# Gated attention, routed experts and a dense layer on one core: the attention's last tiles reordered, embeddings used unscaled, expert weights loaded earlier

## The chip, the cores and the metric

The kernel runs on one core of a Trainium2 chip. The metric is the device time of one execution in microseconds (us), the median of several runs.

## What is computed

The reference has three stages, each feeding the next. Inputs are float32.

```python
# 1. gated recurrent attention: 4 batches x 8 heads, 768 steps, head dim 48
for t in range(S):
    state = alpha[:, :, t, :, None] * state + einsum('bhd,bhe->bhde', k[:, :, t], v[:, :, t])
    y[:, :, t] = einsum('bhd,bhde->bhe', q[:, :, t], state)
x = y.transpose(0, 2, 1, 3).reshape(3072, 384)
# 2. one of 8 experts per token, by cosine
xn = x / (norm(x) + 1e-6); en = expert_emb / (norm(expert_emb) + 1e-6)
logits = xn @ en.T / tau
idx = argmax(logits, 1); gate = softmax(logits)[arange(N), idx]
for e in range(8):                                   # w1: 384 x 1024, w2: 1024 x 384
    m = idx == e; out[m] = gate[m, None] * (maximum(x[m] @ w1[e], 0) @ w2[e])
# 3. dense layer, 384 -> 2048 -> 384, with ELU
h = out @ w_in; g = where(h > 0, h, exp(minimum(h, 0)) - 1); y = g @ w_out
```

## The kernel before, in words

**Attention** (`attention()`, L287) works on 24 tiles: 6 chunks of 128 steps times 4 batches, all heads of a tile together. A tile goes through stages that are pipelined over the loop of `fast()` (L714 on). `stR` (L333) and `stA` (L346) are two scans of the gates on VectorE (DVE), each followed by a product on GpSimd (POOL): Kh (L344) and Qh (L353). `stS` (L372) makes scores on TensorE (PE, 16 matmuls, L381), `stP` (L383) masks them on DVE in two halves, `stT` transposes Kh, `stC_state`, `stC_carry` and `stC_values` make the product with the carried state (L408), the new state (L434) and the product with the values (L426); ScalarE (ACT) evicts. `stD` (L457) multiplies the tile's rows with a matrix rhsX that holds an identity and the expert embeddings, so that one pass gives the token rows and their logits; ACT copies the rows and sums their squares, and DVE reduces the logits (L469; the reduce is kept in a list `late`). In turn `i` of the loop stand: the loads of tile i+4 on SP's queue, the scores of i+1, the scans of i+2, the masks of i+1, pending routing steps (`step(5)`, `step(7)` take up to 12 from a list `todo`), the rows of i-1 and the state and value products of i. PE, DVE, ACT and POOL take their instructions in the order in which the program writes them.

**Start.** `fast()` loads the tiles' gates (`at`), q and k in one piece (`qk`), v, the constants (`cs`), the embeddings (`emb_t`) and the matrix `sel` from which rhsX is broadcast. The embeddings are normed by 15 small steps (`inv_norm1`, L129: two on DVE, then twelve Newton steps and an addition on ACT, L140 to L148, with reciprocals on DVE at L705 and L732), scaled on ACT (L733, L734), transposed on PE (L762) and copied into rhsX (L763), in turn 0.

**Routing.** The tiles form six groups (0 to 5, 6 to 11, 12 to 15, 16 to 19, 20 and 21, 22 and 23). For a group, `stR1` (L495) takes maximum, one-hot and counts of the logits on DVE, with the inverse norm of the rows (`inv_norm`, L106) beside it; `stR2` (L547) turns counts into row numbers by small matmuls (L553 to L557) and three DVE steps; `stX` and `gates` make the softmax weight; `put` (L578) scales a tile's rows on ACT (L574, L575) and scatters them by an indirect DMA of POOL (L584) into a buffer `xs` in DRAM, sorted by expert.

**Weights.** The expert weights come in pieces of 128 x 512. `load_w` loads one, `split_piece` (L189) splits it into a high part (ACT, L201) and a low part (DVE, L204). Twelve pieces, expert 0's whole weight, are loaded and split during attention, from tile `WAIT` on; the low parts of eight of them are put off (`spare`, run by `split_spare`). The dense layer's weights are 64-bit words, loaded by `load_d` and decoded by `decode` (L228) on DVE, ACT and POOL during the expert stage.

**Ending.** After turn 21, `ending()` (L808) writes out by hand the order of the last tiles, the last groups' routing, the packing of the counts, the test of the decays and the first expert's input: tiles 22 and 23 are put straight into its first layer by a product with one-hot columns (`first_x`, L592), the other rows are read back from `xs` on SP's queue (`load_rows`) and transposed (`turn`, L967, L982).

**Experts** (`moe1`, L955): 8 experts of 8 blocks, one first-layer product and one second-layer product per block; after the first two blocks a branch (L1058) chooses the common path by a number that all engines read. Behind it stand `load_d(0)`, `load_d(1)`, `load_x(1)`. The last block's `mm2` evicts its outputs to `x2T` (L1041, L1042, L1045) and splits the first 512 columns for the dense layer in between (`split_x`, L1103). **Dense layer** (`moe2`, L1151): 6 units of 512 tokens, 16 blocks each: h (L1187) into one of four PSUM banks, then minimum, exp, ELU and the split into gh and gl on DVE and ACT (L1189 to L1197), then the output product (L1208 to L1210), which for the last term needs gl.

Of the kernel before, what the change touches and what calls it, by code (L numbers as in the profile page):

```python
# [8 lines left out]
F32 = mybir.dt.float32  # L9
# [31 lines left out]
WAIT = 10  # L41
# [18 lines left out]
CONST = [("ident", 128), ("tri", 128), ("dec", E), ("base", E), ("tok", NT), ("key", E), ("cap", E), ("iota", E)]  # L60
# [3 lines left out]
def fused_kernel(ctx, tc, qk, a, v, emb, w12, wi, wo, cst, sel, cols, out):  # L64
# [38 lines left out]
    ss = const.tile([128, NT], F32, name="ss")  # L103
    tick = const.tile([1, 1], F32, name="tick")
# [24 lines left out]
    def inv_norm1(pool, x):  # L129

        shape = [x.shape[0], 1]
        y = pool.tile(shape, F32, name="rs_y1")
        t = pool.tile(shape, F32, name="rs_t1")
        h = pool.tile(shape, F32, name="rs_h1")
        yi, vec, act = y.bitcast(I32), nc.vector, nc.scalar
        first = [
            lambda: vec.tensor_scalar(yi, x.bitcast(I32), 1, None, op0=ALU.logical_shift_right),
            lambda: vec.tensor_scalar(yi, yi, -1.0, float(0x5F3759DF), op0=ALU.mult, op1=ALU.add),
        ]
        steps = [lambda: act.activation(out=h, in_=x, func=AF.Copy, scale=-0.5)]  # L140
        for _ in range(3):
            steps += [
                lambda: act.activation(out=t, in_=y, func=AF.Copy, scale=h),
                lambda: act.activation(out=t, in_=t, func=AF.Copy, scale=y),
                lambda: act.activation(out=t, in_=t, func=AF.Copy, bias=1.5),
                lambda: act.activation(out=y, in_=t, func=AF.Copy, scale=y),
            ]
        steps += [lambda: act.activation(out=y, in_=y, func=AF.Copy, scale=x, bias=1e-6)]  # L148
        return y, first, steps

# [23 lines left out]
    def split_spare(n):  # L174

        for _ in range(n):
            if spare:
                spare.pop(0)()
# [10 lines left out]
    def split_piece(lag=None):  # L189
# [13 lines left out]
        def low_part():  # L203
            nc.vector.tensor_tensor(l[:, sl], r, h[:, sl].bitcast(F32), op=ALU.subtract)  # L204
# [82 lines left out]
    def attention():  # L287
        with ExitStack() as st:
# [27 lines left out]
            def load(i):  # L316
# [3 lines left out]
                at[i], qkt[i] = ats[i % LB], qks[i % LB]  # L320
# [136 lines left out]
            def stD(i, keep=False):  # L457
# [23 lines left out]
                if keep:  # L481
                    late.pop()()
# [181 lines left out]
            def fast():  # L664
# [38 lines left out]
                for f in guess:  # L703
                    f()
# [632 lines left out]
```

## Time and profile before

| | |
|---|---|
| runs | 796.0, 794.42, 794.0 us; median 794.42 |
| profiled execution | 795.59 us, span 793.8 us |
| PE busy | 770.1 us, 97% of the span |
| DVE busy | 522.2 us, 66% |
| ACT busy | 362.6 us, 46% |
| POOL busy | 188.9 us, 24% |
| granted TensorE clock | 0.992 of full speed on the whole |
| DMA | 76.25 MB, 96 GB/s over the span |

The span is the time between the first and the last instruction of the profiled execution; the execution's own time is 1.79 us longer. Attention takes the first 130 us or so, its ending reaches to 160, the experts to 385, the dense layer to the end. Busy shares are means over these stages. In a timeline, the bracket behind an instruction says how long its engine stood idle before it and what the profile names as the releaser.

### The profile page before, as it was taken

What the parts mean: (1) busy time and instruction counts of PE and PEld (TensorE: products, weight loads), DVE (VectorE), ACT (ScalarE), POOL (GpSimd) and SP (SyncE); (2) the same over time, 40 slices, a digit from 0 to 9 for tenths busy, and PEclk for the clock granted to TensorE, in tenths of its full rate; (3) what the DMA queues carried; (4) which work ended last, traced back from release to release, by engine and by line L of the source; (5) the groups of instructions that cost most, each with busy time, mean ns of one, the idle gap of its engine ahead of it and who ended that gap; (6) DMA issues with size and microseconds to landing.
All of it is one profiled execution on the core that took longest, in us unless ns stands there. A gap on an engine that the chain in (4) does not pass through costs nothing.

```text
span 793.8 us, 13698 instructions
## 1 busy us (share of the span) xinstructions
PE 770.1 (97%) x5077; PEld 699.1 (88%) x5077; DVE 522.2 (66%) x1001; ACT 362.6 (46%) x802; POOL 188.9 (24%) x222
## 2 busy tenths in 40 slices
PE   7999998899999999999999999999999999999996
PEld 4888887489999999999898899999999999999996
DVE  6789999846877877896576755454555545545442
ACT  4667877435455455554545433333333323323231
POOL 5545667322333433342000020020002002002002
PEclk9899999999999999999999999999999999999999
DMA  9998773366665666661000010010001001001001
GB/s 245 245 259 205 233 202 92 109 176 201 185 198 184 204 198 204 213 200 35 1 1 1 1 40 1 0 40 1 1 1 40 1 1 40 1 0 41 1 1 40
DMA packets 44804, 76.25 MB, mean 96 GB/s; under 512 B 11958, under 2 KB 21302, under 8 KB 44734
## 3 DMA queue, kind: packets, MB, share of 16 engines
q1 hardware_dynamic: 41662, 65.89, 29.5%
q0 software_dynamic: 3072, 9.45, 3.3%
q8 instruction: 40, 0.66, 0.4%
q14 instruction: 30, 0.25, 0.1%
HBM read 63.12 MB, written 12.22 MB: 95 GB/s over the span
## 4 chain that ended last, share of the span: by engine, by line
PE 40%; issue 30%; DVE 3%; POOL 3%; ACT 2%; POOLq 0%; ACTq 0%
PE h L1187 6%; PE y L1031 5%; PE y L1033 4%; PE y L1032 4%; PE h L1000 4%; PE h L1001 4%; PE h L999 4%; POOL out_dram L1221 2%; PE o L1210 2%; PE o L1208 2%; PE o L1209 2%; PE t L980 1%; DVE dlo L260 1%; DVE g L1193 1%; DVE mn L1189 1%
## 5 line engine op out<-in xcount | busy, mean ns | idle before, releaser
L1189 DVE TENSOR_SCALAR mn<-h 128x512 f32<-128x512 f32 x96 | 66.2, 690 | 139.7 <-PE h L1187 139.7
L1190 ACT ACTIVATE mn<-mn 128x512 f32<-128x512 f32 x96 | 60.7, 632 | 171.7 <-DVE mn L1189 163.2
L1210 PE MATMUL o<-dwo,gl 128*128 128x384 f32 x384 | 129.4, 337 | 1.4 <-DVE gl L1197 1.4
L1209 PE MATMUL o<-dlo,gh 128*128 128x384 f32 x384 | 128.4, 334 | 0.0
L1208 PE MATMUL o<-dwo,gh 128*128 128x384 f32 x384 | 128.2, 334 | 0.0
L1187 PE MATMUL h<-xh,dwi 128*128 128x512 f32 x288 | 112.8, 392 | 0.6 <-ACT x2T L1045 0.6
L1187 PE MATMUL h<-xh,dlo 128*128 128x512 f32 x288 | 113.2, 393 | 0.0
L1187 PE MATMUL h<-xl,dwi 128*128 128x512 f32 x288 | 112.5, 392 | 0.0
L1221 POOL DMA_INDIRECT out_dram<-ob,ids x24 | 23.2, 965 | 340.8 <-ACT ob L1218 337.1
L1196 ACT ACTIVATE gh<-g 128x512 fp32r<-128x512 f32 x96 | 60.7, 633 | 77.9 <-DVE g L1193 77.9
L1003 ACT ACTIVATE hh<-h 128x432 fp32r<-128x432 f32 (+6 forms) x64 | 32.4, 506 | 107.1 <-PE h L1001 98.9
L204 DVE TENSOR_TENSOR wlo<-raw,whi 128x512 fp32r<-128x512 f32 x96 | 72.8, 786 | 5.6 <-ACT whi L201 5.6
L1193 DVE SCALAR_TENSOR_TENSOR g<-mn,h 128x512 f32<-128x512 f32 x96 | 66.1, 688 | 15.2 <-ACT mn L1190 14.7
L1208 PEld LDWEIGHTS o<-dwo,gh 128*128 128x128 f32 x384 | 72.0, 187 | 4.2
L1209 PEld LDWEIGHTS o<-dlo,gh 128*128 128x128 f32 x384 | 72.0, 187 | 4.0
L1210 PEld LDWEIGHTS o<-dwo,gl 128*128 128x128 f32 x384 | 72.2, 188 | 2.1 <-DVE gl L1197 1.7
L1004 DVE SCALAR_TENSOR_TENSOR hl<-h,hh 128x432 fp32r<-128x432 f32 (+6 forms) x64 | 36.7, 574 | 48.8 <-ACT hh L1003 47.4
L1031 PE MATMUL y<-hh,whi 128*128 128x432 f32 (+6 forms) x192 | 68.3, 356 | 0.0
L999 PE MATMUL h<-xh,whi 128*128 128x432 f32 (+6 forms) x192 | 66.5, 346 | 0.7 <-ACTq L1058 0.7
L244 POOL TENSOR_SCALAR dg<-dg 128x384 f32<-128x384 f32 x32 | 41.7, 1304 | 106.3 <-ACT dg L243 106.1
L1197 DVE TENSOR_TENSOR gl<-g,gh 128x512 fp32r<-128x512 f32 x96 | 65.7, 684 | 1.2 <-ACT gh L1196 1.1
L1001 PE MATMUL h<-xh,wlo 128*128 128x432 f32 (+6 forms) x192 | 66.4, 346 | 0.0
(217 smaller groups left out, 1508.9 us busy)
## 6 DMA issues: line engine op xcount, KB each, us to landing
raw<-in_w_dram SPq DMA_DIRECT2D x96, 256.0 KB
qk<-in_qk_dram SPq DMA_DIRECT2D x40, 192.0 KB
raw<-in_wi_dram SPq DMA_DIRECT2D x16, 384.0 KB
raw<-in_wo_dram SPq DMA_DIRECT2D x16, 384.0 KB
vt<-in_v_dram SPq DMA_DIRECT2D x24, 192.0 KB
xr<-xs SPq DMA_DIRECT2D x7, 576.0 KB
at<-in_alpha_dram SPq DMA_DIRECT2D x40, 99.0 KB
xs<-zero SPq DMA_DIRECT2D x7, 288.8 KB
```

The source lines that it names most:

```text
L204: nc.vector.tensor_tensor(l[:, sl], r, h[:, sl].bitcast(F32), op=ALU.subtract)
L999: nc.tensor.matmul(ps, wh, xh[:, kk], start=(kk == 0), stop=False)
L1001: nc.tensor.matmul(ps, wl, xh[:, kk], start=False, stop=(kk == KD - 1))
L1031: nc.tensor.matmul(acc[e][d], wh, hh, start=(f == 0), stop=False)
L1187: nc.tensor.matmul(ps, l, x, start=(n == 0), stop=(n == len(terms) - 1))
L1189: nc.vector.tensor_scalar(mn, ps, 0.0, None, op0=ALU.min)
L1190: nc.scalar.activation(out=mn, in_=mn, func=AF.Exp)
L1193: nc.vector.scalar_tensor_tensor(g, mn, -1.0, ps, op0=ALU.add, op1=ALU.max)
L1197: low.append(lambda: nc.vector.tensor_tensor(gl, g, gh.bitcast(F32), op=ALU.subtract))
L1208: nc.tensor.matmul(o_, gh[:, sl], wh, start=(f == 0), stop=False)
L1209: nc.tensor.matmul(o_, gh[:, sl], wl, start=False, stop=False)
L1210: nc.tensor.matmul(o_, gl[:, sl], wh, start=False, stop=(f == M - 1))
```

## The change

At the start the embeddings come unscaled as part of `sel` and go into rhsX with it; `emb`, its norm and its transposes go. The norm of the embeddings and 1/tau are made later (squares of rhsX on ACT and a sum by a matmul with ones at tile 2, one reduce and 16 more DVE steps put into `todo` at tile 5), and each group's logits are multiplied by them (`en`) in `stR1`. The loads are reordered and q and k of tile 0 split; in the first four turns the scan A stands ahead of both masks. `WAIT` goes from 10 to 9. `ending()` has a new order. Two of the last seven spare low parts stay on DVE and five go to POOL. In `moe1`, `load_x(1)` is issued ahead of the loads of the 64-bit weights, their decoding starts two blocks later, and the first dense input is split ahead of the last block's `mm2`. In `moe2`, h uses the three banks of `psG`, which stays open, in place of its own four; the first block's products are no longer reordered. The core of the diff:

```diff
-WAIT = 10
+WAIT = 9
...
-    def inv_norm1(pool, x):
...
-    def split_spare(n):
+    def split_spare(n, eng=None):
 
         for _ in range(n):
             if spare:
-                spare.pop(0)()
+                spare.pop(0)(eng)
...
-        def low_part():
-            nc.vector.tensor_tensor(l[:, sl], r, h[:, sl].bitcast(F32), op=ALU.subtract)
+        def low_part(eng=None):
+            (eng or nc.vector).tensor_tensor(l[:, sl], r, h[:, sl].bitcast(F32), op=ALU.subtract)
...
-                y = ys[i] = psG.tile([128, NP, T], F32, tag="g", name="psY") if i == NT - 1 else ps1.tile([128, NP, T], F32, name="psY")
+                y = ys[i] = psG.tile([128, NP, T], F32, tag="g", name="psY") if i == NT - 2 else ps1.tile([128, NP, T], F32, name="psY")
...
                 nc.scalar.activation(out=sq, in_=rows, func=AF.Square, accum_out=ss[:, i:i + 1])
-                if keep:
-                    late.pop()()
...
                 ops = [
+                    lambda: nc.vector.tensor_tensor(l, l, en.to_broadcast(s3), op=ALU.mult),
                     lambda: nc.vector.tensor_reduce(mx, l, axis=AX.X, op=ALU.max),
...
+                if g == NG - 3:
+                    return pz[:, 128:128 + 8 * E].rearrange("p (n e) -> p n e", e=E)
...
             def fast():
...
-                emb_t = sm.tile([E, 2 * NP * HP + 1], F32, bufs=1, name="emb_t")
-                load(0)
+                ones_f = wk.tile([128, 128], F32, bufs=1, tag="ones_f", name="ones_f")
+                esq = sm.tile([128, NP, E], F32, bufs=1, name="esq")
+                es = sm.tile([128, E], F32, bufs=1, name="es")
+                load(0, True)
+                load_a(1)
+                load_k(1)
                 nc.sync.dma_start(out=cs, in_=cst)
-                nc.sync.dma_start(out=emb_t, in_=emb)
-                load(1)
+                load_a(2)
                 load_v(0)
-                load(2)
-                nc.sync.dma_start(out=rhsX, in_=sel[:, None, :].to_broadcast([128, NP, CW + E]))
+                load_k(2)
+                nc.sync.dma_start(out=rhsX, in_=sel)
                 load_v(1)
                 load(3)
                 load_v(2)
...
-                rows, rtau = emb_t[:, :2 * NP * HP], emb_t[:, 2 * NP * HP:]
-                es = sm.tile([E, 1], F32, name="es")
-                esq = wk.tile([E, 2 * NP * HP], BF16, bufs=1, tag="junk", name="esq")
-                en, guess, newton = inv_norm1(sm, es)
+                nc.gpsimd.memset(ones_f, 1.0)
                 for j in range(2):
                     stR(j)
                     stA(j)
                     stH(j)
-                    if j == 0:
-                        stE(j)
-                        nc.scalar.activation(out=esq, in_=rows, func=AF.Square, accum_out=es)
+                    stE(j)
                 stS(0)
                 stT(0)
-                warm(ps1, "psY", 4)
-                for f in guess:
-                    f()
-                nc.vector.reciprocal(rtau, rtau)
-                stE(1)
+                warm(ps1, "psY", 6)
                 stP(0, 0)
                 stP(0, 1)
-                for f in newton:
-                    f()
+                inv, norms = inv_norm(sm, es)
+                norms += [
+                    lambda: nc.vector.reciprocal(c["tau"], c["tau"]),
+                    lambda: nc.vector.tensor_tensor(en[:, 0], inv, c["tau"].to_broadcast([128, E]), op=ALU.mult),
+                ]
...
                     stR(i + 2)
-                    stP(i + 1, 0)
-                    if i == 0:
-                        nc.vector.reciprocal(en, en)
-                        nc.scalar.activation(out=rows, in_=rows, func=AF.Copy, scale=en)
-                        nc.scalar.activation(out=rows, in_=rows, func=AF.Copy, scale=rtau)
-                    stA(i + 2)
-                    stP(i + 1, 1)
+                    if i < B:
+                        stA(i + 2)
+                        stP(i + 1, 0)
+                        stP(i + 1, 1)
+                    else:
+                        stP(i + 1, 0)
+                        stA(i + 2)
+                        stP(i + 1, 1)
+                    if i == 5:
+                        todo.append(lambda: nc.vector.tensor_reduce(es, sums, axis=AX.X, op=ALU.add))
+                        todo.extend(norms)
...
                         m, n = stR1(last[i - 2])
+                        todo.append(m.pop(0))
...
                     if i == 0:
-                        eT = psD.tile([128, NP, E], F32, tag="psX", name="eT")
-                        for p in range(NP):
-                            nc.tensor.transpose(eT[:, p], rows[:, p * 128:(p + 1) * 128], c["ident"][:E, :E])
-                        nc.scalar.activation(out=rhsX[:, :, CW:CW + E], in_=eT, func=AF.Copy)
+                        warm(psD, "psX", 3)
+                    if i == 2:
+                        nc.scalar.activation(out=esq, in_=rhsX[:, :, CW:CW + E], func=AF.Square)
+                        nc.tensor.matmul(pz[:, 64:64 + NP * E], ones_f, esq.rearrange("p n e -> p (n e)"), start=True, stop=True)
+                        sums = pz[:, 64:64 + NP * E].rearrange("p (n e) -> p e n", n=NP)
...
             def ending():
...
                     put(putq.pop(0))
+                stC_state(i)
+                stS(i + 1)
+                stC_values(i)
                 stD(i - 1)
-                stS(i + 1)
+                late.pop(0)()
+                run(todo)
+                todo.clear()
+                x3 = stX(g3)
                 stP(i + 1, 0)
                 stP(i + 1, 1)
                 late.pop(0)()
-                r = stR2(g2 - 1)
-                run(todo, r)
-                todo.clear()
-                stC(i)
-                x3 = stX(g2 - 1)
-                split_spare(2)
-                run(x3 + gates(g2 - 1), late)
-                late.clear()
-                gated.add(g2 - 1)
+                stC_state(i + 1)
+                stD(i, True)
+                r = stR2(g3)
+                stC_values(i + 1)
+                run(x3 + gates(g3), r)
+                gated.add(g3)
+                late.pop(0)()
+                for _ in range(2):
+                    put(putq.pop(0))
+                stD(i + 1, True)
                 m2, n2 = stR1(g2)
                 run(m2, n2)
-                for _ in range(2):
-                    put(putq.pop(0))
-                stC(i + 1)
-                stD(i, True)
+                late.pop(0)()
                 r = stR2(g2)
                 x2 = stX(g2)
-                run(r, x2 + gates(g2))
-                split_spare(1)
-                stD(i + 1, True)
                 while putq:
                     put(putq.pop(0))
+                run(r, x2 + gates(g2))
                 warm(ps1, "psY", 8)
                 for j in GROUPS[g2]:
                     put(j)
+                split_spare(1)
                 xr = xr_p.tile([128, 4, DM], F32, name="xr")
                 load_rows(xr, 0, [0, 128, 256, DM], puts[:-1])
...
-                split_spare(5)
+                split_spare(2)
+                split_spare(5, nc.gpsimd)
                 return xr, t0
...
                     y = acc.pop(e)
-                    if e == E - 1:
-                        for nm in ("xh2", "xl2"):
-                            first.append([stage.tile([128, U], F32R, tag="raw", name=nm) for _ in range(KD)])
                     nc.scalar.activation(out=x2T[:, 0, bass.ds(o1, n)], in_=y[0], func=AF.Copy)
                     nc.vector.tensor_copy(x2T[:, 1, bass.ds(o2, n)], y[1])
-                    if first:
-                        split_x(x2T, *first, 0, 0)
                     nc.scalar.activation(out=x2T[:, 2, bass.ds(o1, n)], in_=y[2], func=AF.Copy)
-                    if first:
-                        split_x(x2T, *first, 0, 1)
-                        split_x(x2T, *first, 0, 2)
...
+                load_x(1)
                 load_d(0, dc)
                 load_d(1, dc)
-                load_x(1)
...
+                    if n == len(blocks):
+                        for nm in ("xh2", "xl2"):
+                            first.append([stage.tile([128, U], F32R, tag="raw", name=nm) for _ in range(KD)])
+                        for kk in range(KD):
+                            split_x(x2T, *first, 0, kk)
                     if n >= LAG:
                         mm2(*blocks[n - LAG])
...
-                    j = (n - 2) * 4 // 7
-                    if j >= 0 and j != (n - 3) * 4 // 7:
+                    j = (n - 4) * 3 // 5
+                    if j >= 0 and j != (n - 5) * 3 // 5:
                         decode(j, dc, dense)
...
-            psH = st.enter_context(tc.tile_pool(name="psH2", bufs=4, space=PS))
...
-                ps = psH.tile([128, U], F32, name="h2")
+                ps = psG.tile([128, U], F32, tag="g", name="h2")
...
-                if u == f == 0:
-                    terms = [terms[n] for n in (0, 1, 3, 4, 6, 7, 2, 5, 8)]
```

## Rows read from the trace of the kernel before

**Rows 1.** Busy time by stretch; after each engine (x) instructions; then clock, DMA share, GB/s

```profile
0.00:20.00 20.00, 15.78 (x118) 9.51 (x119) 12.62 (x24) 9.25 (x28) 10.71 (x21) 0.93 0.95 244
...
120.00:165.00 45.00, 37.46 (x341) 28.29 (x339) 36.27 (x163) 24.74 (x77) 22.65 (x36) 0.96 0.41 126
165.00:384.00 219.00, 218.81 (x1203) 211.47 (x1203) 163.54 (x274) 107.84 (x217) 74.26 (x64) 1.00 0.57 173
...
390.00:450.00 60.00, 58.63 (x293) 52.15 (x292) 41.42 (x71) 29.98 (x58) 0.20 (x1) 1.00 0.05 1
```

**Rows 2.** Timeline, 7 to 24 us: start, duration, engine, line, [idle before <-releaser]

```profile
7.21 1.25 DVE L341 TENSOR_TENSOR_SCAN R<-at,pz 112x528 f32<-112x528 f32 x1 [0.89 <-DMA at<-in_alpha_dram]
...
8.45 1.16 PE L381 MATMUL psS<-Qh,Kh 48*128 48x128 f32 x16
...
11.36 1.23 DVE L341 TENSOR_TENSOR_SCAN R<-at,pz 112x528 f32<-112x528 f32 x1
...
14.90 0.15 DVE L732 RECIPROCAL rs_y<-rs_y 8x1 f32<-8x1 f32 x1 [1.42 <-ACT rs_y L148]
14.98 1.25 DVE L351 TENSOR_TENSOR_SCAN A<-at,pz 112x528 f32<-112x528 f32 x1
...
17.65 2.08 PE L381 MATMUL psS<-Qh,Kh 48*128 48x128 f32 x16 [0.53 <-POOL Qh L353]
...
22.29 1.94 PE L426 MATMUL psY<-P,vt 128*64 128x128 f32 x16
```

**Rows 3.** Waits, 38 to 54 us: total us, times, longest

```profile
DVE P L388 <- PE psS L381: 4.3, 3, 1.4
```

**Rows 4.** DVE groups by form, 55 to 130 us: busy us, mean ns

```profile
L518 DVE TENSOR_TENSOR lg<-lg,rs_y 128x48 f32<-128x48 f32 x2 | 1.2, 606 | 0.1
...
L119 DVE TENSOR_TENSOR rs_t<-rs_t,rs_y 128x6 f32<-128x6 f32 x6 | 1.0, 161 | 0.1
```

**Rows 5.** Timeline of POOL and of DVE around one tile

```profile
85.42 1.27 POOL L353 TENSOR_TENSOR Qh<-qk,A 112x512 f32<-112x512 f32 x1 [0.87 <-DVE A L351]
...
86.29 0.47 DVE L509 TENSOR_TENSOR e__1387<-lg,mx 128x48 f32<-128x48 f32 x1
```

**Rows 6.** Timeline of PE, the ending of attention and the start of the experts

```profile
135.84 0.19 PE L553 MATMUL psR<-base,ident 128*128 128x32 bf16 x1 [1.48 <-DVE lg L469]
...
136.09 1.42 PE L408 MATMUL psY<-Qh,G 48*64 48x128 f32 x16
137.44 1.98 PE L426 MATMUL psY<-P,vt 128*64 128x128 f32 x16
...
140.72 1.09 PE L426 MATMUL psY<-P,vt 128*64 128x128 f32 x16
...
150.49 3.17 PE L596 MATMUL t<-hot,xt 128*128 128x432 f32 x8 [1.40 <-ACT xt L574]
...
160.32 0.46 PE L999 MATMUL h<-xh,whi 128*128 128x432 f32 x1
...
164.78 0.47 PE L999 MATMUL h<-xh,whi 128*128 128x432 f32 x1 [0.67 <-ACTq L1058]
```

**Rows 7.** Timeline of POOL, the same stretch

```profile
141.82 0.95 POOL L584 DMA_INDIRECT xs<-xt,pos_i  x1 [4.39 <-ACT xt L575]
...
149.95 1.04 POOL L584 DMA_INDIRECT xs<-xt,pos_i  x1 [0.23 <-issue]
...
159.25 0.96 POOL L584 DMA_INDIRECT xs<-xt,pos_i  x1 [8.18 <-DVE xl L1022]
```

**Rows 8.** Timeline of DVE, the same stretch

```profile
154.07 3.08 DVE L204 TENSOR_TENSOR wlo<-raw,whi 128x512 fp32r<-128x512 f32 x5
158.02 0.61 DVE L1022 TENSOR_TENSOR xl<-t,xh 128x432 fp32r<-128x432 f32 x1 [0.88 <-ACT xh L1021]
```

**Rows 9.** Timeline, 383 to 392 us, and the page's group of L1210

```profile
386.39 0.50 PE L1187 MATMUL h<-xh,dwi 128*128 128x512 f32 x1 [0.59 <-ACT x2T L1045]
...
L1210 PE MATMUL o<-dwo,gl 128*128 128x384 f32 x384 | 129.4, 337 | 1.4 <-DVE gl L1197 1.4
```

More of the change, by code (lines that the diff above doesn't have):

```diff
@@ L103, in fused_kernel @@
     ss = const.tile([128, NT], F32, name="ss")
+    en = const.tile([128, 1, E], F32, name="en")
     tick = const.tile([1, 1], F32, name="tick")
@@ L127, in inv_norm @@
         return y, steps
-    def inv_norm1(pool, x):
[L131 to L149, printed above, removed]
     wq = [(e, s) for e in range(E) for s in range(FB * FW // SLOT)]
@@ L314, in seg, with load, load_a @@
                 return t.rearrange("c (p t) -> c p t", t=TP)
-            def load(i):
+            def load(i, apart=False):
+                load_a(i)
+                load_k(i, apart)
+            def load_a(i):
                 if i >= NT:
@@ L319, in load, with load_k @@
                 cc, b = divmod(i, B)
-                at[i], qkt[i] = ats[i % LB], qks[i % LB]
-                for t, src in ((at[i], a), (qkt[i], qk)):
-                    for r in [slice(0, C2)] if i < LB else [slice(0, D), slice(HP, C2)]:
-                        nc.sync.dma_start(out=t[r], in_=src[cc, r, b])
+                at[i] = ats[i % LB]
+                for r in [slice(0, C2)] if i < LB else [slice(0, D), slice(HP, C2)]:
+                    nc.sync.dma_start(out=at[i][r], in_=a[cc, r, b])
+            def load_k(i, apart=False):
+                if i >= NT:
+                    return
+                cc, b = divmod(i, B)
+                t = qkt[i] = qks[i % LB]
+                for r in [slice(0, C2)] if i < LB else [slice(0, D), slice(HP, C2)]:
+                    for n in [slice(1, 2), slice(0, 1)] if apart else [slice(0, 2)]:
+                        nc.sync.dma_start(out=t[r, n], in_=qk[cc, r, b, n])
             def load_v(i):
@@ L1254, in fused_kernel @@
     psG = shared.enter_context(tc.tile_pool(name="psG", bufs=3, space=PS))
-    xr_p = shared.enter_context(tc.tile_pool(name="xr", bufs=1, side="right"))
+    rest = ExitStack()
+    xr_p = rest.enter_context(tc.tile_pool(name="xr", bufs=1, side="right"))
     x0 = attention()
@@ L1259, in fused_kernel @@
         first, dense = moe1(x2T, *x0, es)
-        shared.close()
+        rest.close()
         with tc.manual_schedule():
             moe2(x2T, first, dense)
+        shared.close()
 _OUTS = [((N, DM), "float32")]
@@ L1307, in _layout @@
         "cap": np.broadcast_to(np.array(CAPS)[None, :], (128, E)),
+        "tau": np.broadcast_to(np.asarray(inputs["moe_tau"], np.float32).reshape(1, 1), (128, 1)),
         "iota": np.broadcast_to(np.arange(E)[None, :], (128, E)),
```

18 lines of the change are left out of this document (8 added, 10 removed).

## The prediction

> **What bounds the kernel now.** I read the page first: PE is busy 97% of the span, so a gain must come from stretches where PE stands or runs slowly. The windows say which [rows 1]: from 165 to 384 us PE works 218.81 of 219.00, so the expert stage has nothing to give. The first 20 us hold 4.2 us without PE work at a granted clock of 0.93; 120 to 165 (the last tiles, the routing, the first expert's input) holds 7.5 at 0.96; the 60 us after the change of stages hold 1.4, nearly all of it one stall [rows 1, 9]. The timeline of the first stretch comes next. VectorE (DVE) stands 1.42 us until ScalarE has finished its Newton steps on the embeddings; only then come L732 and tile 2's scan A, and its scores start at 17.65 [rows 2]. They take 2.08 us where tile 0's took 1.16, and a values product at 22.29 takes 1.94 where a later one takes 1.09: PE there runs at about its lower level, after having stood idle [rows 2, 6]. In the middle of attention PE leads and DVE has slack: 4.3 us in 16 us, three times for the scores [rows 3]. In the ending, PE waits 1.48 for a reduce of DVE before the row counts, the next values product is slow (1.98), and GpSimd (POOL), which scatters the rows, waits 4.39 for scaled rows, so that its last early scatter starts at 149.95; the first expert's first product then starts at 160.32 [rows 6, 7]. The working below goes against the profiled run, 795.59 us (span 793.8 and 1.79 around it); that is 1.17 above the median of 794.42.
>
> **The change part by part.** *Start.* Removed are two dozen small operations on the embeddings, among them L732. Scan R(2) began at 11.36 for 1.23 us, behind R(1), which waited 0.89 for its load [rows 2]; that load is now issued ahead of the constants. I put R(2) some 0.7 earlier, at 10.65, and A(2), which now comes right behind it, at about 12.0: 3.0 us earlier than 14.98. The two masks that A passes (tile 1's) are delayed by about its 1.25, and PE with them; so of the 3.0 I count 2.5 at the scores of tile 2. With PE kept at work by the longer warm-up and without the hole, scores and values give back up to 0.92 and 0.85, if the clock stays up; a product of the rows between them should give as much. That makes 2.5 to 5.1 at the loop's middle; I take 4.5, since the holes that I can see ahead of the slow products go, but masks arrive later. Below 2.5 lies a start whose loads set the pace: the stretch has a DMA share of 0.95 [rows 1], so I keep 1 as the lower end.
>
> *Operations put into the loop.* Seventeen small ones (14 of the inverse norm, a reduce, a reciprocal, a product) come in tiles 5 and 6. The same kind of step takes 0.16 [rows 4]: 2.8 us, against two tiles with about 1.4 of slack each [rows 3]. This hides all but the first one of each tile, if it is held: L509 takes 0.47 and ends at 86.76, just after POOL's Qh, which runs from 85.42 to 86.69 [rows 5]. I take 0.5 net (0 to 2). The product with the norms, new in each group, falls four times in a loop that DVE nearly fills. Its price lies between 0.16, a step, and 0.61, L518 [rows 4]; it takes the place in front of L509, where the hold falls, so I take 0.3, 1.2 in all (0.6 to 2.4). Here the rule of the Trainium skill, "SBUF — State Buffer", section "SBUF: two separate sides", speaks against the change: a DVE operation with two SBUF inputs and a GpSimd operation that reads SBUF exclude each other for a whole instruction; the row of L509 agrees (0.47, ending where POOL ends). By it a held product would push L508 and L509 back by 0.4 a time, 1.6 in all, and the sum would be 0.4 us less gain.
>
> The expert pieces one tile earlier are as many loads, copies and subtractions as before; what is dropped from tile 21 is put into tile 9. I count nothing: POOL's queue sees no piece, and SP issues one load earlier, behind the loads of its tile. Without that cover, one subtraction held by POOL costs 0.6 more. The one matmul and the square at tile 2 are under 0.3 us on engines with room.
>
> *The ending.* The state and values products of tile 22 come ahead of the counts that wait for DVE. This fills the 1.48 with the state product's 1.42; with the hole gone, the values product may come back from 1.98 to 1.09, so PE is 1.4 to 2.4 earlier at the last tile [rows 6]. The masks of the last tile, though, now stand behind the remaining routing steps on DVE, and the scatters behind ScalarE's scalings: POOL's queue moves as a whole, its six early scatters in the order they had. By walking the new order with the rows' durations I get the last of them at 147.8, not 149.95 [rows 7]. Behind it wait SP's load of the gathered rows and the transposes; beside them lies PE's work for the first tile of expert 0 (from 150.49 [rows 6]), which does not move as far. I take 1.7 at the start of the experts (0 to 2.2; 0 if the masks behind the routing steps give it all back).
>
> *Five low parts on GpSimd.* Before, five subtractions took 3.08 on DVE, ending 0.88 before its next work [rows 8]: hidden. Two stay there, five go to POOL at 1.27 each by the size of Qh [rows 5], 6.4 us, behind the last two scatters, from about 159 to 166. First use is the second half of expert 0, four blocks of 3.5 us (219.00 us over 62 blocks [rows 1]) behind its start, so I price it at 0; without that cover it is a rival below. SP: the two row loads ahead of the four pieces of 64-bit weights, the decode two blocks later: hidden by a stage in which the rows show no wait; if one piece came late, up to one such block, 3.5.
>
> *Between the stages.* PE stood 0.59 for an eviction L1045, and its first product then took 0.50 [rows 9], as those do that start when their operands come. Splitting the rows a block earlier puts three ScalarE copies ahead of the evictions, so they end later, but the split itself is done when PE comes. The hole and 0.4 for such products make 1.0 at most; a chain on DVE that lags until the stall of L1210, 1.4 [rows 9], swallows part. I take 0.4 (0 to 1). Three PSUM buffers in place of four for h: the buffer is read two steps ahead of the low part that PE already waits for, so I count 0; the lower end is half the stall again, 0.7.
>
> Sum: 4.5 − 0.5 − 1.2 + 1.7 + 0.4 = 4.9. 795.59 − 4.9 = 790.7, which against the median is 789.5.
>
> **Rivals.** *A, the start gives little:* PE still falls to its low level and the masks behind A eat the rest; start 2.0, all else as above: gain 2.4, 792.0. For it: the masks do move back, and POOL's 1.27 per product sets Qh. Against: the 1.42 and L732 are removed outright.
>
> *B, the added DVE steps are held by POOL (slower):* at L518's 0.61, 21 steps in the loop cost 12.8, less 2.8 of slack, so 10.0; against 4.5 + 1.7 + 0.4 that is 3.4 slower, 797.8. It decides from 9.4/21 = 0.45 a step. For it: L518's and L509's rows, and the small room of DVE. Against it: six steps L119 of the same kind at 0.161, because one POOL instruction holds one step, not all.
>
> *C, GpSimd's low parts hold the experts' start:* if PE's first product, or the branch at 164.78 where PE already waits for ScalarE's sequencer [rows 6], had to wait for POOL at 166, the 158.6 planned for the first product becomes up to 165.7: 7.1 lost, 2.2 slower in the net, 796.6; half of it gives 793. Against: PE waits for ScalarE there, and POOL is in no row of that wait.
>
> *D, it does not do what it says:* the ending's wait moves to the masks of tile 23 and the start is eaten by loads: within 1 us of before, 794.4.
>
> **How the numbers follow.** A difference of 0.3% (2.4 us) is about what a measurement here can tell from none. Forecast 0.66 (its own range 787 to 792), A 0.12, B 0.08, C 0.07, D 0.07. Faster: the forecast and 0.05 of A, 0.71. Same: the rest of A (0.07), D (0.07) and 0.02 of C, 0.16. Slower: B and 0.05 of C, 0.13. For the range: the best ends (start 5.1, norms 0, product 0.6, ending 2.2, between 1.0) give 7.7, 786.7; above, it takes in A and D and leaves out B and most of C: 786.5 to 795.5.
>
> **What would show it.** Right: scan A of tile 2 near 12 us, tile 2's sixteen scores from about 15 in 1.2 us, all later scans R 2.5 to 4 us earlier; no 1.48 before the counts; the last early scatter near 145 (147.8 less the loop's gain of 2.8); the first h some 4.5 earlier; five low parts on POOL with nobody waiting for them; h of the dense layer without the 0.59. Wrong: slow scores at tile 2 again, DVE with less idle time and yet later at tile 12, PE waiting for POOL in the first expert, or a new wait for psG in the dense layer.

## The result: slower, and the profile after

The changed kernel takes 800.02 us (median of 4 runs, 799.31 to 801.96) beside 794.21 for the kernel before (4 runs): ratio 1.0087, 95% interval 1.0063 to 1.0111. That is 5.0 to 8.8 us slower, and the medians lie 5.8 apart. The range of the prediction ended at 795.5, and its sum had the other sign. The profiled run after took 799.31 with a span of 797.3; against the profile of before that is 3.5 us of span, and those 3.5 can be followed through the trace. The rest of the 5.8 is the choice of runs: the profile shown of before (795.59) is one of its slower runs, as e9 and e12 below show, and that of the change is the fastest of its four.

The windows of the kernel after, same columns as in [rows 1], with one more window behind the branch:

```profile
0.00:20.00 20.00, 16.53 (x127) 9.73 (x128) 14.01 (x22) 4.36 (x10) 10.90 (x23) 0.91 0.92 227
120.00:165.00 45.00, 35.39 (x336) 26.73 (x335) 32.82 (x160) 23.13 (x75) 28.78 (x41) 0.99 0.39 123
165.00:384.00 219.00, 217.97 (x1181) 209.96 (x1182) 163.81 (x272) 107.32 (x216) 74.66 (x64) 0.99 0.56 173
390.00:450.00 60.00, 58.31 (x285) 50.95 (x284) 41.65 (x72) 30.11 (x58) 0.33 (x1) 1.00 0.05 1
165.00:172.00 7.00, 6.18 (x18) 5.37 (x19) 1.12 (x2) 0.70 (x2) 0.00 (x0) 0.55 0.45 128
```

The window from 120 to 165 us holds 9.6 us without PE work where it held 7.5, and POOL works 28.78 in place of 22.65. Behind it stand 7 us at a mean granted clock of 0.55. The timeline of PE, POOL and ACT in this stretch says what happened (the rows answer to [rows 6, 7]):

```profile
135.42 1.09 PE L400 MATMUL psY<-Qh,G 48*64 48x128 f32 x16
...
137.41 0.18 PE L546 MATMUL pz<-base,ident 128*128 128x32 bf16 x1
...
148.61 3.17 PE L589 MATMUL t<-hot,xt 128*128 128x432 f32 x8 [1.28 <-DVE hot L857]
...
157.49 0.47 PE L999 MATMUL h<-xh,whi 128*128 128x432 f32 x1
...
165.80 0.73 PE L999 MATMUL h<-xh,whi 128*128 128x432 f32 x1 [4.49 <-ACTq L1050]
...
168.15 0.56 PE L1001 MATMUL h<-xh,wlo 128*128 128x432 f32 x1
...
173.88 0.35 PE L999 MATMUL h<-xh,whi 128*128 128x432 f32 x1
...
147.26 0.96 POOL L577 DMA_INDIRECT xs<-xt,pos_i  x1
...
158.52 6.19 POOL L183 TENSOR_TENSOR wlo<-raw,whi 128x512 fp32r<-128x512 f32 x5
...
164.75 0.95 ACT L1003 ACTIVATE hh<-h 128x432 fp32r<-128x432 f32 x2 [6.62 <-POOL wlo L183]
```

Before, the first eviction hh and the first product of the fourth block were these:

```profile
162.39 0.53 ACT L1003 ACTIVATE hh<-h 128x432 fp32r<-128x432 f32 x1 [1.43 <-PE h L1001]
...
170.65 0.36 PE L999 MATMUL h<-xh,whi 128*128 128x432 f32 x1
```

The first product of the experts starts at 157.49, 2.83 earlier than in the shown profile of before (how much of this is the new ending, e8, e9 and e12 ask). But the first eviction hh stands 6.62 us on ACT until the last of GpSimd's five low parts ends at 164.71; ACT reaches the branch only behind it, and PE, which needs ACT there, stands 4.49. Then its products take 0.73 and 0.56 us in place of 0.36. The fourth block, at 170.65 before, starts at 173.88.

The same blocks, followed to the end, give the whole difference. At tile 22's scan R the two kernels are level (122.39 and 122.33). At the first block the change is 2.83 ahead, at the fourth 3.23 behind (6.06 lost at the branch); in expert 6 it loses 0.4 more, where PE has a wait of 0.2 for DVE's hl that before has not; at the second block of the dense layer it is 2.64 behind (1.04 won at the transition), 3.51 from block 14 on (0.9 given back), and 3.51 at the end.

The start, timeline as in [rows 2]:

```profile
8.22 1.25 DVE L333 TENSOR_TENSOR_SCAN R<-at,pz 112x528 f32<-112x528 f32 x1 [1.79 <-DMA at<-in_alpha_dram]
...
9.72 1.25 DVE L343 TENSOR_TENSOR_SCAN A<-at,pz 112x528 f32<-112x528 f32 x1
...
10.50 0.76 PE L357 MATMUL psT<-cs,Kh 112*128 112x112 f32 x4 [1.23 <-DMA cs<-in_cst_dram]
10.89 1.26 DVE L380 TENSOR_TENSOR P<-psS,cs 128x512 f32<-128x512 f32 x2
...
11.05 2.77 PE L264 MATMUL warm<-ones 128*128 128x512 bf16 x6
...
12.07 1.24 DVE L333 TENSOR_TENSOR_SCAN R<-at,pz 112x528 f32<-112x528 f32 x1
...
13.66 1.25 DVE L343 TENSOR_TENSOR_SCAN A<-at,pz 112x528 f32<-112x528 f32 x1
...
14.11 1.28 POOL L336 TENSOR_TENSOR Kh<-qk,R 112x512 f32<-112x512 f32 x1 [1.58 <-DMA qk<-in_qk_dram]
...
17.81 1.16 PE L373 MATMUL psS<-Qh,Kh 48*128 48x128 f32 x16
...
26.30 0.41 PE L758 MATMUL pz<-esq,ones_f 128*128 128x32 f32 x2 [0.47 <-ACT esq L757]
...
26.80 1.25 DVE L333 TENSOR_TENSOR_SCAN R<-at,pz 112x528 f32<-112x528 f32 x1 [2.18 <-PE pz L758]
```

The slow products of tile 2 are gone: 1.16 where [rows 2] have 2.08. But the scores start no earlier, although scan A of tile 2 does by 1.3. R(1) stands 1.79 for its load instead of 0.89; PE stands 1.23 for the constants, and the six filling products behind that take 2.77 (1.46 in e2, below); and POOL's Kh of tile 2 stands 1.58 for the load of q and k, so that Qh, which comes behind it, ends 1.7 behind the scan. Three filling products, written ahead of the scores, are the last thing before them. A new wait stands at 26.80: every scan reads a column of the PSUM tile pz as its floor, and the sums of the squared embeddings are written into another column of pz, so scan R of tile 5 stands 2.18 behind that product. At tile 7's scores the change is 2.45 ahead (41.74 against 44.19); ahead of tile 8's scan come the norm steps (POOL and DVE, columns as in [rows 2]):

```profile
39.53 1.27 POOL L345 TENSOR_TENSOR Qh<-qk,A 112x512 f32<-112x512 f32 x1 [2.16 <-DVE A L343]
...
40.26 0.57 DVE L114 TENSOR_SCALAR rs_y<-es 128x8 int32<-128x8 int32 x1
40.87 0.17 DVE L115 TENSOR_SCALAR rs_y<-rs_y 128x8 int32<-128x8 int32 x1
...
51.40 1.29 POOL L345 TENSOR_TENSOR Qh<-qk,A 112x512 f32<-112x512 f32 x1 [0.60 <-DVE A L343]
...
52.04 0.72 DVE L498 TENSOR_TENSOR lg<-lg,en 128x48 f32<-128x48 f32 x1
```

The first step ends at 40.83, just after Qh at 40.80, and takes 0.57 where the next takes 0.17; the product with the norms takes 0.72 and ends at 52.76, just after Qh at 52.69. Each is held by the POOL instruction in progress.

### The profile page after: what moved, and what is told of

Read it like the earlier page. It is cut to its first block, busy times and chain, and to the rows that moved or that the text cites. A ratio compares the mean times of both kernels' runs of the same rounds, so it can differ in the third digit from the quotient of the medians.

```text
span 797.3 us, 13715 instructions
## 1 busy us (share of the span) xinstructions
PE 769.9 (97%) x5080; PEld 697.8 (88%) x5080; DVE 526.4 (66%) x1015; ACT 357.7 (45%) x784; POOL 196.3 (25%) x228
## 4 chain that ended last, share of the span: by engine, by line
PE 37%; issue 31%; DVE 5%; ACT 3%; POOL 2%; DMA 0%; POOLq 0%; ACTq 0%; DVEq 0%
PE h L1181 5%; PE y L1031 4%; PE h L999 4%; PE h L1000 4%; PE y L1032 4%; PE h L1001 4%; PE y L1033 4%; POOL out_dram L1215 2%; PE o L1204 2%; PE o L1202 2%; PE o L1203 2%; DVE dlo L239 2%; PE t L980 1%; DVE g L1187 1%; DVE mn L1183 1%
## 5 line engine op out<-in xcount | busy, mean ns | idle before, releaser
L1004 DVE SCALAR_TENSOR_TENSOR hl<-h,hh 128x432 fp32r<-128x432 f32 (+6 forms) x64 | 36.6, 573 | 54.3 <-ACT hh L1003 53.9
L1000 PE MATMUL h<-xl,whi 128*128 128x432 f32 (+6 forms) x192 | 67.0, 349 | 0.0
```

What stands on the lines that cost most here:

```text
L1000: nc.tensor.matmul(ps, wh, xl[:, kk], start=False, stop=False)
```

## The experiments

Ratios are against runs of the kernel before on the same chip. Positions are starts in the one profile of each run.

**e1, no low part on GpSimd.**

```diff
-                split_spare(2)
-                split_spare(5, nc.gpsimd)
+                split_spare(7)
```

> The changed kernel with all seven late low parts on VectorE, none on GpSimd. Theory (the first eviction hh waits for the last of GpSimd's five subtractions; PE then stands 4.49 us at the branch and runs at the lower clock behind it): the wait goes, expert 0's fourth block starts at about 167.9 instead of 173.88 in the profile, and the time falls by 6.0 us, to about 794. Rival (the wait at the branch comes from the new order of the ending or of the loads): the fourth block stays near 173.9 and the time near 800.

Measured: 792.21 us, ratio 0.9982 (0.9967 to 0.9996). The fourth block starts at 167.71. PE at the branch has its old wait:

```profile
161.83 0.46 PE L998 MATMUL h<-xh,whi 128*128 128x432 f32 x1 [0.67 <-ACTq L1049]
...
167.71 0.36 PE L998 MATMUL h<-xh,whi 128*128 128x432 f32 x1
```

With the five subtractions on DVE the whole loss goes; the order of the ending and of the loads, which stay, have no part in it. From the first block to the fourth it takes 10.37 us (167.71 less 157.34), as before (10.33); the change takes 16.39.

**e2, GpSimd keeps its five low parts, their inputs in a pool of their own.**

```diff
-            early_p.append(st.enter_context(tc.tile_pool(name="early", bufs=AHEAD * PIECES - DIRECT)))
+            early_p.append(st.enter_context(tc.tile_pool(name="early", bufs=5)))
+            early_p.append(st.enter_context(tc.tile_pool(name="early3", bufs=3)))
...
-                pool = early_p[0] if DIRECT <= nload[0] < AHEAD * PIECES else stage
+                pool = early_p[int(nload[0] < DIRECT + 3)] if DIRECT <= nload[0] < AHEAD * PIECES else stage
```

> The changed kernel with the five subtractions still on GpSimd, but the pieces that they read lie in a buffer pool of their own, below the three that VectorE splits, so that the buffers of hh take over memory of the second pool only. Theory (hand-over of memory: hh waits because its pool takes over the memory of the whole pool of early pieces): as with no low part on GpSimd, 6.0 us faster than the change, about 794, fourth block at about 167.9, five subtractions on GpSimd still there from about 158.5 to 164.7. Rival (GpSimd's subtractions block VectorE or ScalarE themselves, through a shared port or through the weights they make): time stays near 800, fourth block near 173.9.

Measured: 791.92 us, ratio 0.9987 (0.9972 to 1.0003), fourth block at 167.09. POOL, PE and ACT:

```profile
157.59 6.27 POOL L183 TENSOR_TENSOR wlo<-raw,whi 128x512 fp32r<-128x512 f32 x5
...
161.21 0.47 PE L1000 MATMUL h<-xh,whi 128*128 128x432 f32 x1 [0.67 <-ACTq L1051]
...
167.09 0.36 PE L1000 MATMUL h<-xh,whi 128*128 128x432 f32 x1
...
158.81 0.53 ACT L1004 ACTIVATE hh<-h 128x432 fp32r<-128x432 f32 x1 [1.43 <-PE h L1002]
```

The same subtractions run at the same place for 6.27 us, and the eviction at 158.81 now waits for PE alone. From the first block to the fourth it takes 10.35 us (the first starts at 156.74), as before. So the subtractions do not block ScalarE or VectorE, nor are their results missed: what held hh is the hand-over of memory. The only edit is where GpSimd's inputs lie, and the pool of hh takes over memory of the early pieces' pool when that one is closed. Whether hh waited for the last user of the old pool as a whole, or only for pieces that lie under its own bytes, no run shows: e2 moves the pieces and splits the pool at once.

**e3, the kernel before with its five low parts on GpSimd**, nothing else.

```diff
-                split_spare(5)
+                split_spare(5, nc.gpsimd)
```

> The kernel before with only one edit: its last five low parts on GpSimd. Theory: GpSimd has the last two scatters until about 161.5, so the five end at about 167.8; the eviction hh, at 162.39 before, waits for that; the third block starts at about 169 instead of 164.78, and slow products follow; 6 to 7 us slower, about 801. Rival (the hold needs the new ending): no change, 794.

Measured: 800.03 us, ratio 1.0093 (1.0064 to 1.0122).

```profile
160.03 6.20 POOL L204 TENSOR_TENSOR wlo<-raw,whi 128x512 fp32r<-128x512 f32 x5
...
167.31 0.73 PE L999 MATMUL h<-xh,whi 128*128 128x432 f32 x1 [4.66 <-ACTq L1058]
```

This one edit alone makes the kernel before as slow as the whole change does, and at the same place: from the first block (158.85) to the fourth (175.32) it takes 16.47 us, where the change takes 16.39.

**e4, the change with filling products at the branch.**

```diff
                 for f in range(EARLY):
                     mm1(0, f)
+                warm(psG, "g", 22)
```

> The changed kernel with 22 idle-filling products (128x512, results unused) behind expert 0's second block, so that PE works while the branch waits for GpSimd. Theory: the wait itself stays (third block near 165.8), but the block and the two second-layer products behind it run at 0.36 us a product instead of 0.56, so the fourth block starts some 2.2 us earlier than 173.88, near 171.7, and the time is 2 us less than the change's, near 798. Rival (the slow products come from something else, contention with the loads behind the branch): still 0.56 a product, fourth block at 173.9.

Measured: 796.31 us (one run), fourth block at 170.80. The window behind the branch, columns as in [rows 1]:

```profile
165.00:172.00 7.00, 7.00 (x36) 6.33 (x35) 1.08 (x2) 0.53 (x1) 0.00 (x0) 1.00 0.58 171
```

The clock stays at 1.00 where the change has 0.55, as expected. The time alone does not give the price, since e4's first block already starts 1.12 us earlier (156.37). From the second block to the fourth the change takes 14.51 us, e4 12.55, e1 8.48: of the 6.03 lost, 4.07 are the wait and 1.96 the low clock that follows it. This split is good to some 0.3 us: e4's third block starts 0.36 behind the end of ScalarE's evictions, the change's 0.10, so a little of the 4.07 is the filling products themselves.

**e5, e2 without the norms of the embeddings.**

```diff
-                    if i == 5:
-                        todo.append(lambda: nc.vector.tensor_reduce(es, sums, axis=AX.X, op=ALU.add))
-                        todo.extend(norms)
...
-                        todo.append(m.pop(0))
...
-                    lambda: nc.vector.tensor_tensor(l, l, en.to_broadcast(s3), op=ALU.mult),
```

> The kernel with two pools, with the norm of the embeddings and the products with it left out (17 steps in turns 5 and 6 and one product per group; the logits stay unscaled). Theory (the start's 2.45 us of gain at tile 7 goes to these VectorE steps): scan R of tile 8 near 40.0 instead of 42.85, and scores of tile 22 near 124.6 instead of 127.01, that is 2.4 earlier; the first expert block 2.4 earlier than with two pools. Rival (the loads set the pace from tile 8 on, so the gain would be lost anyway): scores of tile 22 stay within 0.5 of 127.0.

Measured: 788.53 us (one run). R(8) at 39.59 and R(22) at 118.57, where e2 has 42.66 and 121.96: 3.4 earlier, more than the 2.4 expected. DVE waits for the scores again, 1.43 a turn, as it did before:

```profile
42.48 0.69 DVE L381 TENSOR_TENSOR P<-psS,cs 128x512 f32<-128x512 f32 x1 [1.43 <-PE psS L374]
```

The norm steps and products are the sink of the start's gain; the loads are not. With its logits unscaled, tokens can go to other experts, so only its positions inside attention are read here, not its time.

**e6, e2 with the sums in a PSUM tile of psX's kind and reduced at once.**

```diff
-                        nc.tensor.matmul(pz[:, 64:64 + NP * E], ones_f, esq.rearrange("p n e -> p (n e)"), start=True, stop=True)
+                        sums = psD.tile([128, NP, E], F32, tag="psX", name="sums")
+                        nc.tensor.matmul(sums, ones_f, esq, start=True, stop=True)
+                        late.append(lambda: nc.vector.tensor_reduce(es, sums.rearrange("p n e -> p e n"), axis=AX.X, op=ALU.add))
```

> The kernel with two pools, with the sums of the squared embeddings in a PSUM tile of their own (and reduced at once) and not in pz, of which every scan reads a column. Theory (the scan of tile 5 stood 2.18 us because it waits for that product in pz): R(5) at about 24.6 instead of 26.80, no idle time in front of it; since PE leads from tile 5 on, tile 7's scores gain 0.3 to 0.9 and tile 22's at most 0.5. Rival (R(5) waits for its buffer or its load): R(5) stays at 26.8.

Measured: 792.71 us (one run). The scan is freed, but another wait takes its place:

```profile
24.77 1.25 DVE L334 TENSOR_TENSOR_SCAN R<-at,pz 112x528 f32<-112x528 f32 x1 [0.42 <-DMA at<-in_alpha_dram]
...
28.82 0.18 DVE L760 TENSOR_REDUCE es<-sums 128x8 f32<-128x32 f32 x1
...
29.05 1.11 PE L457 MATMUL psX<-rhsX,yT 128*128 128x104 f32 x8 [1.13 <-DVE es L760]
```

The two buffers of psX are needed every turn; one of them now waits for the reduce, PE stands 1.13, and R(22) is 0.7 later than in e2 (122.67). The wait on pz was real, but this was no way out.

**e7, e6 with the norm steps spread over turns 3 to 5, and rhsX's embedding columns multiplied once in turn 6**, so that only the first group multiplies its logits.

```diff
-                    if i == 5:
-                        todo.extend(norms)
+                    if 3 <= i < 6:
+                        todo.extend(norms[(i - 3) * 6:(i - 2) * 6])
...
+                    if i == 6:
+                        es_ = rhsX[:, :, CW:CW + E]
+                        nc.vector.tensor_tensor(es_, es_, en.to_broadcast([128, NP, E]), op=ALU.mult)
```

> As e6, and the 16 norm steps in three portions in turns 3 to 5, where VectorE waits for the scores, and rhsX's embeddings scaled once in turn 6, so that only the first group multiplies its logits. Theory: most of the 2.4 us of the norm steps comes back without leaving anything out: scores of tile 22 near 125 instead of 127.0, the time 1.5 to 2.5 us under that of two pools, near 790, 0.4 to 0.6% under before. Rival (VectorE's backlog is the same wherever the steps stand): within 0.5 us of two pools, 792.

Measured: 791.14 us, ratio 0.9984 (0.9969 to 0.9999). R(22) is at 119.74, 2.2 earlier than in e2, of the 3.4 that e5 gives. Against before it stands hardly better than e2 (0.9984 and 0.9987), so the time does not show what the trace does: 0.16% under before, where 0.4 to 0.6% was expected.

**e8, the kernel before with the new order of the ending alone**: of the diff, the hunks of `ending()`, `stD`, `count_tile` and the PSUM buffer of `stC_state`, with

```diff
-                split_spare(5)
+                split_spare(7)
```

> The kernel before with the new order of the ending only (all low parts on VectorE, old start, old stages behind). Theory (the new order is worth what the trace of the change shows between tile 22 and the first block): first block at about 157.5 instead of 160.32, 2.8 us faster than before, near 791.3. Rival (that gain belongs to the low parts leaving the routing stretch or to the earlier pieces): under 1 us.

Measured: 790.65 us, ratio 0.9964 (0.9947 to 0.9980), 2.4 us less by the medians. Its profile is of a run of 793.6, and there the first block is at 158.32, 0.8 later than expected, and the eight products L596 take 5.55 us instead of 3.17. The time carries the verdict, not this one trace: the new ending is worth having by itself. Of the rival, the earlier pieces are ruled out (`WAIT` stays at 10); the two low parts that leave the routing stretch are a part of this edit, so their share is not told apart from that of the order.

**e9 and e12, the kernel before twice more.**

> The kernel before, unchanged, profiled once more. The profile shown of before took 795.59 us, the median of the runs beside the experiments 793.1 to 793.9. Theory (the start's loads and clock vary from run to run, and the shown profile has a slow start): scans of tiles 1 to 5 and of tile 22 start up to 2 us earlier than 7.21, 28.25 and 122.39 in a run near 793, with the same durations behind. Rival (the difference lies elsewhere, in the dense stage): the start repeats within 0.3 us.

> The kernel before, unchanged, a third look, for the same question as e9: if the start varies, its scans R(1), R(5) and R(22) differ from the other two profiles of before by up to 2 us; if not, all three agree within 0.3 us.

Measured: 793.13 and 792.78 us. R(1) starts at 8.12 and 7.22, R(5) at 27.68 and 26.83 (shown profile: 28.25), R(22) at 121.83 and 120.99 (122.39), the first block at 157.93 and 157.55 (160.32). So only part of the 2.4 to 2.8 us lies in the start, 0.6 and 1.4; the rest lies in the ending, where e9 has the products of [rows 6] all at 1.09:

```profile
135.52 1.09 PE L408 MATMUL psY<-Qh,G 48*64 48x128 f32 x16
136.54 1.09 PE L426 MATMUL psY<-P,vt 128*64 128x128 f32 x16
```

The granted clock from 128 to 150 us is 1.00 in e9 and 0.92 in the shown profile. The dense stage repeats within 0.1. Of the 2.77 us that the change's trace gains between R(22) and the first block, 1.4 to 1.8 belong to the shown run of before.

**e10, as e7, with squares and sums already in turn 0, in pz.**

```diff
                     stC_state(i)
+                    if i == 0:
+                        nc.scalar.activation(out=esq, in_=rhsX[:, :, CW:CW + E], func=AF.Square)
                     stT(i + 1)
+                    if i == 0:
+                        nc.tensor.matmul(pz[:, 64:64 + NP * E], ones_f, esq.rearrange("p n e -> p (n e)"), start=True, stop=True)
```

> As e7 (two pools, norm steps spread over turns 3 to 5, rhsX scaled once), but the squares and their sums are made in turn 0, in pz, behind the transposes of tile 1, where ScalarE is idle, so that neither a scan nor a row product waits for them. Theory: R(5) near 24.5 without idle time and no 1.13 us stand of the row product as with a tile of their own: scores of tile 5 near 30.3 instead of 31.12, tile 22's scan near 119.0 instead of 119.74; 0.5 to 1 us less than e7, about 790.3, 0.3% under before. Rival (PE leads from tile 5 on and swallows it): as e7, 791.1.

Measured: 794.97 us, ratio 1.0008 (0.9994 to 1.0022): a miss. The product stands ahead of scan R(2) in the program, and it needs rhsX, whose load ScalarE awaits until 15.18:

```profile
15.18 0.23 ACT L716 ACTIVATE esq<-rhsX 128x32 f32<-128x32 f32 x1 [3.21 <-DMA rhsX<-in_sel_dram]
...
15.96 1.25 DVE L334 TENSOR_TENSOR_SCAN R<-at,pz 112x528 f32<-112x528 f32 x1 [3.67 <-PE pz L719]
```

**e11, e8 with the change's edits to the expert and dense stages**: of the diff, also the hunks of `moe1`, `mm2`, `moe2` and of the pools around them.

> The kernel before with the new ending and the change's edits to both expert and dense stages (loads, decode schedule, split ahead of the last block, three banks for h), old start, all low parts on VectorE. Theory (the stages behind give 1.0 at the transition and lose 0.9 in the dense layer's first blocks and 0.5 in expert 6): within 0.5 us of e8, about 790.5. Rival (the transition's gain stays): 1 us under e8, 789.6.

Measured: 792.69 us, ratio 0.9979 (0.9965 to 0.9993), beside 0.9964 of e8; the intervals overlap. In its profile, of a run of 795.51, the ending shows no gain at all: from R(22) to the first block it takes 37.79 us, as the shown before does (37.93), and the eight products L596 take 5.45. In its trace the transition gives 1.07 (from 0.40 behind the shown before in expert 6 to 0.67 ahead at the second dense block) and all but 0.06 of that lead is lost by block 16 of the layer: nothing to keep. Which of these stages' edits gives it back no run separates.

**e13, as e10, with the sums' product written behind the scans of turn 0**: the same product, now behind the masks of that turn.

```diff
                         stA(i + 2)
                         stP(i + 1, 0)
                         stP(i + 1, 1)
...
+                    if i == 0:
+                        nc.tensor.matmul(pz[:, 64:64 + NP * E], ones_f, esq.rearrange("p n e -> p (n e)"), start=True, stop=True)
```

> As e10, but the sums' product is written behind the scans of turn 0, so that scan R(2) no longer stands behind it (in e10 it stood 3.67 us and started at 15.96). Theory (a scan waits for every product into pz that the program writes ahead of it, and for nothing else here): R(2) near 11.5, R(5) near 24.5 without idle time, scores of tile 5 near 30.3, tile 22's scan near 119.2; about 790.5, 0.3 to 0.5% under before. Rival (the sums cost their place wherever they stand): 1 us or more over e7's 791.1.

Measured: 790.65 us, ratio 0.9967 (0.9952 to 0.9982). R(2) at 10.97 and R(5) at 24.30, both without the wait, R(22) at 118.70:

```profile
10.97 1.25 DVE L334 TENSOR_TENSOR_SCAN R<-at,pz 112x528 f32<-112x528 f32 x1
...
24.30 1.24 DVE L334 TENSOR_TENSOR_SCAN R<-at,pz 112x528 f32<-112x528 f32 x1
```

This has all parts of the change, mended, and leaves nothing out: 3.3 us less than before by the medians (793.94 beside it), where the change is 5.8 slower. It is no faster than e8, which has the ending alone.

## Why the prediction was wrong

**The five low parts, priced at 0: the step that failed.** I asked who uses their results (the second half of expert 0, rightly far off) and which of DVE's steps could collide with them, and not who takes over the memory of what they read. Measured: 6.06 us lost at the branch, as e1, e2 and e3 show from three sides. Rival C had place and price nearly right, a hold of PE at the branch by POOL until 166 and 7.1 us lost. I gave it 0.07 because PE's row there names ScalarE; but ScalarE was itself behind the eviction, and the chain of two engines, not the row of PE, was the thing to walk. The price of an idle PE was also incomplete: to the wait of 4.07 came 1.96 at the low clock. That rival C's 7.1 lies so near to 6.06 is in part luck, since it was a wait alone and held no term for the clock.

**The start, 4.5 taken: 2.45 in the trace.** That the slow products would go was right: the clock from 15 to 25 us is 1.00 after and was 0.72 and 0.59. That scan A and the scores of tile 2 come 2.5 to 3 earlier was wrong (13.66 and 17.81 instead of 12.0 and about 15): the load of tile 1, which I put 0.7 earlier, came later, and with it scan A of tile 1, behind which the first masks start at 10.89 instead of 10.17; the constants, moved behind that load, hold PE for 1.23; and the load of tile 2's q and k holds POOL for 1.58. So loads hold the start in three places, which is near the case that I had kept for the lower end. The 2.18 on pz I did not see: I costed that product by its duration on an engine with room and did not list who else touches the tile that it writes.

**Norm steps and products, 0.5 and 1.2 taken: 2.4 in the trace (2.45 ahead at tile 7, 0.06 at tile 22), 3.4 by e5.** The mechanism was as put: the first step of a group is held until POOL's Qh ends, the others take 0.17. The size was off. The slack in front of the masks (1.43 per turn in [rows 3], 1.43 in e5) is used up as soon as the steps delay the next scan, and a delayed scan delays Qh and with it the scores; hiding needs the steps to fit in each turn's slack, and 12 in one turn take 2.8. Spread over three turns, and with the product left to the first group alone, they cost less (e7). The rule that I cited, the Trainium skill, "SBUF — State Buffer", section "SBUF: two separate sides", on the exclusive lock, agrees with the row of L498, which reads two SBUF tiles and ends 0.07 after the POOL instruction does. L114 ends 0.03 after it as well, though it reads one tile only, so the words that I cited do not cover it, and by what rule it is held stays open. GpSimd's low parts read SBUF too; in e2 the steps beside them, xl and hl, which each read one input from PSUM, take 0.61, as in e1 without them.

**The ending, 1.7 taken: 2.77 in the trace.** The last early scatter was put at 147.8 and starts at 147.26. Since e9 and e12 need 36.1 and 36.6 us from R(22) to the first block, the shown before 37.9 and the change 35.2, the gain against these two is 0.9 to 1.4 in the trace, near the forecast. No one trace settles it, since e8 and e11, with the new ending on the old start, need 36.4 and 37.8; e8 has 2.4 in time.

**The transition, 0.4 (0 to 1).** 1.04 at the second block, 0.9 of it given back by block 14, where the stall for gl is 1.6 instead of 1.4 and smaller losses lie on both sides of it. The net, 0.16, is inside the range, and the prediction had said that the chain up to this stall swallows part; which edit does it the runs leave open.

**The sum.** The forecast took 4.9 off. With the terms as measured against the shown profile: 0.06 in the loop, 2.77 in the ending and 0.16 between the stages, less 6.06 at the branch and 0.45 in expert 6, is 3.5 slower, the difference of the spans.

**The reference run.** I took the distance between the profile and the median as an offset of 1.17 that cancels. It does not: it was slow products in the start and the ending, the very things that the change removes, so part of what I counted was not to be had in the median run. At tile 7's scores e9 and e12 stand at 43.63 and 42.77: the change's lead of 2.45 there is 1.9 and 1.0 against them.

## What to carry over

When work is moved to another engine, list beside the users of its results the next owner of the memory that it reads: a pool laid over a closed one can wait for a late reader of the closed pool, on whatever engine (6.06 us here), and a piece of off-path work then stands on the path. Put such inputs into a pool of their own, as e2 does; letting that memory pass to something that is used late should do as well, which no run tried. And when a row shows PE waiting for an engine, ask what that engine waits for.

## What the runs showed that I had not expected

A stand of 4.49 us of PE was followed by some 5 us of slow products (0.73 to 0.56 us instead of 0.36), though PE worked without a hole in them. The granted clock of the 7 us from 165 on was 0.55, near the lower of the two levels, 1.2 GHz; with filling products in the stand it stayed at 1.00. Between runs of the same kernel before, the clock of the start (0.72 and 0.59, or 0.89 and 0.77, or 0.78 and 0.88 in the windows 15 to 20 and 20 to 25 us) and of the ending (0.92 or 1.00) differed, and with them the first block by 2.8 us.
